# Weights of the experts split only at a change of expert, under branches on ScalarE and VectorE

## The chip, the cores and the metric

The kernel runs on one core of one Trainium2 chip. The metric is the time of one execution on the device, in microseconds (us). The engines are named as the profile names them: PE (TensorE, matmuls; PEld is its weight loads), DVE (VectorE), ACT (ScalarE), POOL (GpSimd) and SP (SyncE, which here mostly issues DMAs). A q behind an engine's name is its queue of instructions that do no arithmetic.

## The reference

Three layers in a row, all in float32. In the middle one each token goes to one of eight experts.

```python
# 1. causal attention with decay: 4 x 8 heads, 576 positions, 64 wide
scores = scale * q @ k.T + (cum[:, None] - cum[None, :])   # cum = cumsum(log(f))
x = softmax(where(causal, -1e9, scores)) @ v               # -> (2304, 512)
# 2. mixture of experts, top 1: w1 (8, 512, 1024), w2 (8, 1024, 512)
logits = x @ w_gate + modality_bias[modality_id]
e_idx = argmax(logits, axis=1)
for e in range(8):
    mask = e_idx == e
    h = maximum(x[mask] @ w1[e], 0.0)
    out[mask] = gate_w[mask, None] * (h @ w2[e])           # gate_w: softmax at e_idx
# 3. dense: w_in (512, 2048), w_out (2048, 512)
h = out @ w_in
y = maximum(0.01 * h, h) @ w_out
```

## The kernel before

Every float32 matmul of the last two layers is made of three: an operand is split into a high part (`..h`, rounded to the type that PE takes at full rate) and the rest (`..l`), and high by high, high by low and low by high are summed in PSUM. To split a tile takes a cast on ACT, `hi = raw`, and a subtraction on DVE, `lo = raw - hi`. Tiles are named so: `w1r`, `w1h`, `w1l` are the raw, high and low part of an expert's w1, four pieces of 128x1024 each; `w2r`, `w2h`, `w2l` the same of w2; `xh`, `xl` of the tokens of a slot, `hh`, `hl` of the hidden layer.

The attention runs first, 16 groups in 4 batches of tokens, and each batch is routed as it comes. The expert stage works on slots of 128 tokens of one expert. The first four slots (K1 = 4) are full slots out of the first three batches, so that the stage can begin before the last batch is routed; the other slots are laid out by `finish()` when all counts are known. There are at most 25 slots (NS); steps 0 to 17 are always run, the others under `tc.If(nr > t)`. With these inputs 20 slots run.

`step(t)` holds gemm1 of slot t (24 matmuls, four pieces k of w1), `trh(t-1)`, which transposes the hidden layer of the slot before, `trx`, which transposes the tokens of the next slot, and gemm2 of slot t-1 (24 matmuls). Inside a step the instructions of all five engines keep the order in which the code issues them (`ordered`), except that the work which `finish()` and the last routing issue, outside of it, is put between them by a scheduler with priorities. Each engine runs its own list in order and waits with semaphores.

In before, every step splits the eight weight pieces of the next slot, also where the expert stays the same (`split(t + 1, 0, k)` and `split(t, 1, k)`, L744 and L745). Each split is followed by the DMA of that piece for the slot after (L735), which is skipped when that slot has the same expert: `ei` holds the expert of each slot and `ni` whether it is new. `finish()` builds these tables, the slots (`slots`, `scan`), the stacked index tables (`per_token`, L511 and L513; `table`, L520 and L523) and the token indices of the other slots (L528 to L533: matmuls `tp`, then `tq`, `idt`, `gidx` on DVE), from which POOL gathers tokens (L740).

Of the kernel before, what the change touches and what calls it, by code (L numbers as in the profile page):

```python
# [9 lines left out]
F32 = mybir.dt.float32  # L10
F32R = mybir.dt.float32r
BF16 = mybir.dt.bfloat16
# [25 lines left out]
K1 = 4  # L38
# [9 lines left out]
SP = 2.0  # L48
TE = 3
TX = 3  # L50
RLAG = 8
# [29 lines left out]
def fused(ctx: ExitStack, tc, qk0, qk2, vp, f, mid, wg, mb, w1, w2, w_in, w_out, out):  # L81
# [29 lines left out]
    nc.gpsimd.iota(j128, [[P, NSTAT]], base=0, channel_multiplier=0, allow_small_or_imprecise_dtypes=True)  # L111
    col = cp.tile([P, P], F32, name="col")
    nc.gpsimd.iota(col, [[1, P]], base=0, channel_multiplier=0, allow_small_or_imprecise_dtypes=True)
# [15 lines left out]

    gidx, oidx, ei, ni = ([cp.tile([P, n] + d, I32, name=f"{c}{n}") for n in (K1, N2)] for c, d in (("gidx", []), ("oidx", [2]), ("ei", []), ("ni", [])))  # L130
    nt = cp.tile([P, 1], I32, name="nt")
# [11 lines left out]
    def at_slot(tiles, t):  # L143
        return tiles[t >= K1], t - K1 if t >= K1 else t
# [3 lines left out]
    with tc.tile_pool(name="pst", bufs=PST, space=PSUM) as pst:  # L148
# [351 lines left out]
        def slots(tp, n, inc):  # L500
# [38 lines left out]
        def route1(tp, m):  # L539
# [11 lines left out]
            gi, ef = slots(rt, K1, inc)  # L551
            nw = tp.tile([P, K1], F32, name="nw1")
            nc.vector.memset(nw, 1.0)
            nc.vector.tensor_tensor(nw[:, 1:], ef[:, 1:], ef[:, :K1 - 1], ALU.not_equal)
            nc.vector.tensor_scalar(ei[0], ef, float(E - 1), None, ALU.min)
            nc.vector.tensor_copy(ni[0], nw)
            yield
# [141 lines left out]
    with tc.tile_pool(name="rt2", reuse_waits="tile", bufs=1) as rt2, \  # L699
# [10 lines left out]
        ysc = []  # L710
        R = {}
        for t, c in ((xh, "h"), (xl, "l")):
            t.append(mw.tile([P, DM], F32R, name=f"x{c}1"))
# [4 lines left out]

        def regs(t):
            m, i = at_slot(ei, t)  # L720
            e = nc.sync.value_load(m[0:1, i:i + 1], min_val=0, max_val=E - 1)
# [5 lines left out]
            return e, cnd  # L727

        def load(t, which, k):
            if t not in R:  # L730
                R[t] = regs(t)
            e, cnd = R[t]
            raw, src = (w2r, w2) if which else (w1r, w1)
            o = raw[k].rearrange("p a b -> p (a b)") if which else raw[k]
            nc.sync.dma_start(o, src[bass.ds(e, 1), :, k * FF:(k + 1) * FF].rearrange("o p f -> (o p) f"), cond=cnd)  # L735
# [88 lines left out]
        def step(t):  # L824
            nx = t + 1 < NS
            if not t:
                split(t, 1, 0)
                split(t, 1, 1)
            keepg(t)
            if t == K1 - 1:  # L830
                next(fini)
            if t + 2 < NS and t + 2 != K1:
                gather(t + 2)
            gemm1(t, 0, 2)
            if not t:
                trx(1)
            aside(t, "load")
            if 0 < t < TE:
                trh(t - 1)
            if nx:  # L840
                split(t + 1, 0, 0)
            aside(t, "a1")
            aside(t, "a2")
            if t >= TE:
                trh(t - 1)
            if t > NSTAT:
                split(t - 1, 1, 2)
                split(t - 1, 1, 3)
            aside(t, "b")
            if nx:  # L850
                split(t + 1, 0, 1)
            aside(t, "pool")
            gemm1(t, 2, 3)
            if nx:
                split(t + 1, 0, 2)
            gemm1(t, 3, 4)
            keep(t)
            if nx:
                split(t + 1, 0, 3)
            if t:  # L860
                gemm2(t - 1, 0, 4)
            if nx and 0 < t < TX:
                trx(t + 1)
            if t:
                split(t, 1, 0)
                split(t, 1, 1)
            if nx and t >= TX:
                trx(t + 1)
            if t in (1, K1):
                next(fini, 0)  # L870
            aside(t, "d")
            if t:
                gemm2(t - 1, 4, 8)
            if t < NSTAT:
                split(t, 1, 2)
            if t:
                yout(t - 1)
            if t < NSTAT:
                split(t, 1, 3)

        def finish():
# [9 lines left out]
            gi, ef = slots(rt2, N2, inc)  # L891
            nw = rt2.tile([P, N2], F32, name="nw")
            nc.vector.tensor_tensor(nw[:, 1:], ef[:, 1:], ef[:, :N2 - 1], ALU.not_equal)
            nc.vector.tensor_tensor(nw[:, :1], ef[:, :1], early["ef"][:, K1 - 1:], ALU.not_equal)
            nc.vector.tensor_scalar(ei[1], ef, float(E - 1), None, ALU.min)
            nc.vector.scalar_tensor_tensor(ni[1], ef, float(E), nw, ALU.is_lt, ALU.mult)
# [45 lines left out]
        next(fini)  # L942
        with tc.issue_after(preps[-1].ins):
            for k in range(4):
                load(0, 0, k)
            gather(0)
            gather(1)
            for k in range(4):
                load(0, 1, k)
        with tc.high_priority():  # L950
            for k in range(4):
                split(0, 0, k)
        trx(0)
# [135 lines left out]
```

## Time and profile before

| | us |
|---|---|
| time, median of 3 runs (lowest, highest) | 940.06 (939.44, 940.16) |
| the profiled execution | 940.09 |
| its span | 938.4 |
| attention, about | 0 to 261 |
| steps of the expert stage, about | 261 to 524 |
| dense layer, about | 528 to 938 |
| PE, DVE, ACT, POOL busy | 871.3, 660.1, 504.3, 207.3 |

Times in the views are counted from the start of the span. A timeline row gives start, length, engine, line, operation, tiles and, in brackets, how long the engine idled before it and who released it. [...] Where an instruction overlaps the end of the one before, busy time counts the overlap once.

### The profile page before, as it was taken

What the parts mean: (1) busy time and instruction counts of PE and PEld (TensorE: products, weight loads), DVE (VectorE), ACT (ScalarE), POOL (GpSimd) and SP (SyncE); (2) the same over time, 40 slices, a digit from 0 to 9 for tenths busy, and PEclk for the clock granted to TensorE, in tenths of its full rate; (3) what the DMA queues carried; (4) which work ended last, traced back from release to release, by engine and by line L of the source; (5) the groups of instructions that cost most, each with busy time, mean ns of one, the idle gap of its engine ahead of it and who ended that gap; (6) DMA issues with size and microseconds to landing.
All of it is one profiled execution on the core that took longest, in us unless ns stands there. A gap on an engine that the chain in (4) does not pass through costs nothing. (4 is left out here: it accounts for less than half of the span.)

```text
span 938.4 us, 14476 instructions
## 1 busy us (share of the span) xinstructions
PE 871.3 (93%) x4733; PEld 715.2 (76%) x4733; DVE 660.1 (70%) x1203; ACT 504.3 (54%) x979; POOL 207.3 (22%) x161
## 2 busy tenths in 40 slices
PE   4888888889897999999999999999999999999996
PEld 2766666677676878888878778888888888888885
DVE  8877878679699999999998537348544953483333
ACT  5454555556685889999998445335222532242221
POOL 7433424242011234444443100000000000001112
PEclk9799999899898999999999999999999999999998
DMA  7666757765534842621132124004100420011111
GB/s 203 154 173 177 187 152 173 164 161 123 202 73 135 274 124 72 208 84 47 59 113 92 62 66 135 1 23 115 44 1 1 114 65 1 1 45 45 46 45 68
DMA packets 39754, 94.51 MB, mean 101 GB/s; under 512 B 14108, under 2 KB 14780, under 8 KB 39673
## 3 DMA queue, kind: packets, MB, share of 16 engines
q1 hardware_dynamic: 34872, 78.30, 30.3%
q0 software_dynamic: 4800, 15.23, 5.1%
q8 instruction: 39, 0.64, 0.3%
q14 instruction: 43, 0.34, 0.1%
HBM read 132.08 MB, written 14.99 MB: 157 GB/s over the span
## 5 line engine op out<-in xcount | busy, mean ns | idle before, releaser
L995 DVE SCALAR_TENSOR_TENSOR us<-u,us 128x512 f32<-128x512 f32 (+1 forms) x80 | 51.0, 638 | 125.5 <-ACT us L994 125.0
L994 ACT COPY us<-u 128x512 f32<-128x512 f32 (+1 forms) x80 | 43.5, 544 | 161.8 <-PE u L992 161.7
L992 PE MATMUL u<-fxl,whii 128*128 128x512 f32 (+1 forms) x320 | 118.1, 369 | 0.0
L992 PE MATMUL u<-fxh,wloi 128*128 128x512 f32 (+1 forms) x320 | 117.9, 368 | 0.0
L992 PE MATMUL u<-fxh,whii 128*128 128x512 f32 (+1 forms) x320 | 116.8, 369 | 0.7 <-ACT fxh L650 0.7
L1012 PE MATMUL a<-whio,gh 128*128 128x512 f32 x288 | 112.8, 392 | 0.0
L1012 PE MATMUL a<-wloo,gh 128*128 128x512 f32 x288 | 112.3, 390 | 0.0
L745 DVE TENSOR_TENSOR w1l<-w1r,w1h 128x1024 fp32r<-128x1024 f32 x84 | 101.0, 1223 | 8.5 <-ACT w1h L744 8.2
L1012 PE MATMUL a<-whio,gl 128*128 128x512 f32 x288 | 106.0, 390 | 0.0
L351 ACT ACTIVATE p<-sc,nm 128x128 f32<-128x128 f32 (+3 forms) x128 | 68.0, 535 | 61.1 <-DVE nm L348 48.3
L745 DVE TENSOR_TENSOR w2l<-w2r,w2h 128x1024 fp32r<-128x1024 f32 x80 | 94.4, 1218 | 0.9 <-ACT w2h L744 0.7
L1022 POOL DMA_INDIRECT out<-acc,tid x18 | 17.7, 984 | 327.4 <-DVE acc L1019 290.2
L744 ACT CAST w1h<-w1r 128x1024 fp32r<-128x1024 f32 x84 | 86.1, 1054 | 5.9 <-DMA w1r<-w 3.7
L744 ACT CAST w2h<-w2r 128x1024 fp32r<-128x1024 f32 x80 | 81.4, 1051 | 4.4 <-PE y L792 2.3
L999 DVE TENSOR_TENSOR gl<-us,gh 128x512 fp32r<-128x512 f32 (+1 forms) x80 | 50.9, 637 | 39.7 <-ACT gh L998 38.9
L998 ACT CAST gh<-us 128x512 fp32r<-128x512 f32 (+1 forms) x80 | 46.2, 578 | 58.4 <-DVE us L995 39.7
L792 PE MATMUL y<-w2h,hl 128*128 128x512 f32 x160 | 64.8, 405 | 5.3 <-DVE hl L785 5.3
L992 PEld LDWEIGHTS u<-fxh,whii 128*128 128x128 f32 x320 | 60.2, 188 | 11.1 <-ACT fxh L650 0.9
L992 PEld LDWEIGHTS u<-fxh,wloi 128*128 128x128 f32 x320 | 60.3, 188 | 10.4
L992 PEld LDWEIGHTS u<-fxl,whii 128*128 128x128 f32 x320 | 60.3, 188 | 10.3
L792 PE MATMUL y<-w2h,hh 128*128 128x512 f32 x160 | 66.0, 412 | 0.0
L792 PE MATMUL y<-w2l,hh 128*128 128x512 f32 x160 | 63.9, 399 | 0.0
(262 smaller groups left out, 1945.3 us busy)
## 6 DMA issues: line engine op xcount, KB each, us to landing
w1r<-w SPq DMA_DIRECT2D x88, 512.0 KB
w2r<-w SPq DMA_DIRECT2D x82, 512.0 KB
aq<-hi SPq DMA_DIRECT2D x30, 288.0 KB
rwi<-w_in SPq DMA_DIRECT2D x16, 512.0 KB
rwo<-w_out SPq DMA_DIRECT2D x16, 512.0 KB
raw<-qk SPq DMA_DIRECT2D x14, 576.0 KB
vt<-vp SPq DMA_DIRECT2D x16, 320.0 KB
xr<-yd SPq DMA_DIRECT2D x18, 256.5 KB
```

The costliest lines, as they stand in the source:

```text
L351: nc.scalar.activation(pt[:, :n], view[:, i, :], AF.Exp, bias=nm[:, i:i + 1], scale=1.0, accum_out=sms[g % 3][:, c, j:j + 1])
L744: nc.scalar.copy(hi[k], raw[k])
L745: nc.vector.tensor_tensor(lo[k], raw[k], hi[k].bitcast(F32), ALU.subtract)
L792: nc.tensor.matmul(Yp[t], lhsT=ap[:, k * P:(k + 1) * P], rhs=wp[k // 2][:, k % 2, :], start=(k == 0 and i == 0), stop=(k == NFB - 1 and i ...
L992: nc.tensor.matmul(ps, lhsT=w[:, c], rhs=x[:, k, :], start=(k == 0 and i == 0), stop=(k == NKB - 1 and i == 2))
L994: nc.scalar.copy(us, ps)
L995: nc.vector.scalar_tensor_tensor(us, ps, 0.01, us, ALU.mult, ALU.max)
L998: nc.scalar.copy(gh, us)
L999: nc.vector.tensor_sub(gl, us, gh.bitcast(F32))
L1012: nc.tensor.matmul(A[b][i], lhsT=x[:, c], rhs=w, start=(first and m == 0), stop=(last and m == 2))
L1022: d = nc.gpsimd.indirect_dma_start(out=out[:, :], out_offset=bass.IndirectOffsetOnAxis(ap=tid[:, c:c + 1], axis=0), in_=Y[b, i], in_offset ...
```

## The change

The weights of a slot are split only where its expert differs from that of the slot before. `finish()` and the early routing make flags on the chip: `nwa` (1 where the expert is new), packed into two integers by `bits()` with the powers of two `pw`. ACT and DVE load such an integer into a register and branch on one bit per slot and weight (`resplit`). Inside the branch stand the four splits; the cast of piece 0 is on DVE now, the other three on ACT. Where the branch is not taken, the engine adds to its semaphore what the splits would have added. The raw buffers hold the next other expert of the list (`en`), loaded where `ln` says so, right behind the split that frees them.

In `step`, the splits, which stood one by one between the matmuls, become one `resplit` for w1 of the next slot behind the last gemm1, and one for w2 at the end. `trh(t-1)` comes before the third piece of gemm1 in every step, `trx(t+1)` between the third and the fourth, and gemm2 is issued whole. The tail has no splits. `col`, an input of the routing's one-hot tables `lall`, becomes bf16. The core of the diff:

```diff
-    col = cp.tile([P, P], F32, name="col")
+    col = cp.tile([P, P], BF16, name="col")
...
+        def bits(tp, i, a, b):
+            u = tp.tile([P, b - a], F32, name=f"bu{i}")
+            nc.vector.tensor_tensor(u, nwa[:, a:b], pw[:, :b - a], ALU.mult)
+            r = tp.tile([P, 1], F32, name=f"br{i}")
+            nc.vector.tensor_reduce(r, u, axis=AX.X, op=ALU.add)
+            nc.vector.tensor_copy(nb[i], r)
...
+        def load(t, which, k):
+            raw, src = (w2r, w2) if which else (w1r, w1)
             cnd = None
-            if t:
-                m, i = at_slot(ni, t)
-                n = nc.sync.value_load(m[0:1, i:i + 1], min_val=0, max_val=1)
+            if t < 0:
+                e = first
+            else:
+                if t not in R:
+                    e = nc.sync.value_load(en[0:1, t:t + 1], min_val=0, max_val=E - 1)
+                    R[t] = e, nc.sync.value_load(ln[0:1, t:t + 1], min_val=0, max_val=1)
+                e, n = R[t]
                 cnd = (n != 0)
...
-        def split(t, which, k):
+        def split(which, k):
             raw, hi, lo = (w2r, w2h, w2l) if which else (w1r, w1h, w1l)
-            nc.scalar.copy(hi[k], raw[k])
+            if k == 0:
+                nc.vector.tensor_copy(hi[k], raw[k])
+            else:
+                nc.scalar.copy(hi[k], raw[k])
             nc.vector.tensor_tensor(lo[k], raw[k], hi[k].bitcast(F32), ALU.subtract)
-            if t + 1 < NS:
-                load(t + 1, which, k)
+        def resplit(t, which):
+            p = t >= K1
+            if p not in WD:
+                WD[p] = nc.values_load(nb[p][0:1, 0:1], engines=SPLITTERS, min_val=0, max_val=2 ** (N2 if p else K1) - 1)
+            with tc.If(((WD[p] >> (t - K1 * p)) & 1) != 0):
+                for k in range(4):
+                    split(which, k)
+            for k in range(4):
+                load(t, which, k)
...
             aside(t, "load")
-            if 0 < t < TE:
+            if t:
                 trh(t - 1)
-            if nx:
-                split(t + 1, 0, 0)
             aside(t, "a1")
             aside(t, "a2")
-            if t >= TE:
-                trh(t - 1)
-            if t > NSTAT:
-                split(t - 1, 1, 2)
-                split(t - 1, 1, 3)
+            gemm1(t, 2, 3)
+            if nx and t:
+                trx(t + 1)
             aside(t, "b")
-            if nx:
-                split(t + 1, 0, 1)
             aside(t, "pool")
-            gemm1(t, 2, 3)
-            if nx:
-                split(t + 1, 0, 2)
             gemm1(t, 3, 4)
             keep(t)
+            if not t:
+                for k in range(4):
+                    split(1, k)
+                    load(0, 1, k)
             if nx:
-                split(t + 1, 0, 3)
+                resplit(t + 1, 0)
             if t:
-                gemm2(t - 1, 0, 4)
-            if nx and 0 < t < TX:
-                trx(t + 1)
-            if t:
-                split(t, 1, 0)
-                split(t, 1, 1)
-            if nx and t >= TX:
-                trx(t + 1)
+                gemm2(t - 1, 0, 8)
             if t in (1, K1):
                 next(fini, 0)
             aside(t, "d")
             if t:
-                gemm2(t - 1, 4, 8)
-            if t < NSTAT:
-                split(t, 1, 2)
-            if t:
                 yout(t - 1)
-            if t < NSTAT:
-                split(t, 1, 3)
+                resplit(t, 1)
...
+            bits(rt2, 1, K1, NS)
             nc.vector.tensor_scalar(nt, inc[:, E - 1:E], float(K1), None, ALU.add)
+
+            wn, wx = (rt2.tile([P, NS], F32, name=n) for n in ("wn", "wx"))
+            nc.vector.tensor_scalar(wn, nwa, -BIG, BIG, ALU.mult, ALU.add)
+            nc.vector.tensor_add(wn, wn, efa)
+            nc.vector.scalar_tensor_tensor(wn, slott, float(E), wn, ALU.mult, ALU.add)
+            for a, b in ((0, NS // 2), (NS // 2, NS)):
+                sn = [P, b - a, NS]
+                m = m2.tile([P, XW], F32, tag="ys", name=f"bh{a}")[:, :(b - a) * NS].rearrange("p (t s) -> p t s", s=NS)
+                nc.gpsimd.memset(m, BIG)
+
+                nc.gpsimd.affine_select(m, m, [[1, b - a], [-1, NS]], ALU.is_ge, 0.0, a, 0)
+                nc.vector.tensor_tensor(m, m, wn.unsqueeze(1).to_broadcast(sn), ALU.add)
+                nc.vector.tensor_reduce(wx[:, a:b], m, axis=AX.X, op=ALU.min)
+            nc.vector.tensor_copy(en, wx)
+            nc.vector.tensor_scalar(en, en, E - 1, None, ALU.bitwise_and)
+            nc.vector.scalar_tensor_tensor(ln, wx, BIG, nwa, ALU.is_lt, ALU.mult)
...
         with tc.high_priority():
             for k in range(4):
-                split(0, 0, k)
+                split(0, k)
+        for k in range(4):
+            load(0, 0, k)
         trx(0)
```

What this moves, shown at three places. First DVE where the stage begins. `hl` of slot 0 is what gemm2(0) needs; `h2` is the last table of `finish()`. Before:

```order
L462 TENSOR_REDUCE pf3_3266<-ps_3_3263 128x5 [waits DVE_49]
L886 TENSOR_TENSOR gt_3365<-runb_96,j128_85 128x144 [waits DVE_49]
L785 TENSOR_TENSOR hl_3362<-th0_0_3565,hh_3361 128x512 [waits Activation_49]
L785 TENSOR_TENSOR hl_3362<-th0_1_3572,hh_3361 128x512 [waits Activation_49]
L465 CAST pi3_3269<-pf3_3266 128x5 [waits DVE_49]
L888 TENSOR_REDUCE nsl_3367<-gt_3365 128x8 [waits DVE_49]
L745 TENSOR_TENSOR w1l0_2902<-w1r0_119,w1h0_129 128x1024 [waits DMAHW0_49,Activation_49]
L745 TENSOR_TENSOR w1l1_2903<-w1r1_120,w1h1_130 128x1024 [waits DMAHW1_49,Activation_49]
L466 TENSOR_SCALAR pi3_3269<-pi3_3269 128x5 [waits DVE_49]
L889 TENSOR_TENSOR nsl_3367<-nsl_3367,used_2758 128x8 [waits DVE_49]
L745 TENSOR_TENSOR w1l2_2904<-w1r2_121,w1h2_131 128x1024 [waits DMAHW2_49,PE_49,Activation_49]
L467 TENSOR_SCALAR pi3_3269<-pi3_3269 128x5 [waits DVE_49]
```

After, from the end of `finish()` on (`h2`), with the first branch, that for w1 of slot 1:

```order
L544 TENSOR_TENSOR h2_3438<-h121_3436,idf_94 128x20x21
L774 TENSOR_LOAD en0_105 [waits DVE_49]
L775 REGISTER_ALU x2
L775 COMPARE_AND_BRANCH
L765 CAST w1h0_137<-w1r0_127 128x1024 [waits DMAHW4_49]
L768 TENSOR_TENSOR w1l0_2914<-w1r0_127,w1h0_137 128x1024 [waits DVE_49]
L768 TENSOR_TENSOR w1l1_2915<-w1r1_128,w1h1_138 128x1024 [waits DMAHW5_49,Activation_49]
L768 TENSOR_TENSOR w1l2_2916<-w1r2_129,w1h2_139 128x1024 [waits DMAHW6_49,Activation_49]
L768 TENSOR_TENSOR w1l3_2917<-w1r3_130,w1h3_140 128x1024 [waits DMAHW7_49,Activation_49]
L775 UNCONDITIONAL_BRANCH
L775 UNCONDITIONAL_BRANCH [waits DVE_49]
L817 TENSOR_TENSOR hl_3374<-th0_0_3619,hh_3373 128x512 [waits Activation_49]
```

Before, `hl` of slot 0 stood among the first instructions of `finish()` (`gt`, `nsl`), with the w1 splits of slot 1 after it. Now all of `finish()` up to the table `h2`, and the first branch, stand ahead of it.

Second, PE at the start of gemm1(1); `h1` is its result, `rk` the counts of the last batch. Before:

```order
L764 MATMUL h0_3479<-w1h3_132,xl0_134 128x512 x2
L764 MATMUL h0_3479<-w1l3_2905,xh0_133 128x512 x2
L764 MATMUL h1_3552<-w1h0_129,xh1_3359 128x512 [waits PE_49,Activation_49]
L764 MATMUL h1_3552<-w1h0_129,xh1_3359 128x512
L764 MATMUL h1_3552<-w1h0_129,xl1_3360 128x512 [waits DVE_49]
L764 MATMUL h1_3552<-w1h0_129,xl1_3360 128x512
L764 MATMUL h1_3552<-w1l0_2902,xh1_3359 128x512 [waits DVE_49]
```

After:

```order
L471 MATMUL rk3_3267<-oall_146,onesb_70 128x24
L471 LDWEIGHTS onesb_70
L471 MATMUL rk3_3267<-oall_146,onesb_70 128x16
L775 UNCONDITIONAL_BRANCH
L796 MATMUL h1_3606<-w1h0_137,xh1_3371 128x512 [waits DVE_49,Activation_49]
L796 MATMUL h1_3606<-w1h0_137,xh1_3371 128x512
L796 MATMUL h1_3606<-w1h0_137,xl1_3372 128x512 x2
L796 MATMUL h1_3606<-w1l0_2914,xh1_3371 128x512 [waits DVE_49]
```

Before, the first matmul of `h1` waited for PE and ACT. Now the counts of the last batch come ahead of it, and it waits for DVE too: for the count of pieces that DVE reaches in the first branch, or with the sum that it adds when it passes it.

Third, DVE near the end of the attention, where the first expert's w1 arrives; `xub` is what PE multiplies next. Before:

```order
L523 TENSOR_TENSOR h2_2867<-h14_2865,idf_94 128x15x4
L397 COPY xub_185<-pv13_1_2978 128x192 [waits PE_49]
L408 TENSOR_SCALAR rr14_3169<-sm2_175 128x10 [waits Activation_49]
L409 RECIPROCAL rr14_3169<-rr14_3169 128x10 [waits DVE_49]
L348 TENSOR_REDUCE nm15_0_0_2990<-sc15_0_0_2991 128x2 [waits PE_49]
L745 TENSOR_TENSOR w1l0_2902<-w1r0_119,w1h0_129 128x1024 [waits DMAHW4_49,DMAHW5_49,DMAHW2_49,Activation_49]
```

After:

```order
L544 TENSOR_TENSOR h2_2879<-h14_2877,idf_94 128x15x4
L765 CAST w1h0_137<-w1r0_127 128x1024 [waits DMAHW2_49]
L411 COPY xub_193<-pv13_1_2990 128x192 [waits PE_49]
L422 TENSOR_SCALAR rr14_3181<-sm2_183 128x10 [waits Activation_49]
L768 TENSOR_TENSOR w1l0_2914<-w1r0_127,w1h0_137 128x1024 [waits DMAHW5_49,DMAHW4_49,DVE_49]
L362 TENSOR_REDUCE nm15_0_0_3002<-sc15_0_0_3003 128x2 [waits PE_49]
```

The cast of the first piece, which waits for its DMA, now stands on DVE, ahead of the copy `xub`.

## Rows read from the trace of the kernel before

**Rows 1.** The page: its first two lines.

```profile
span 938.4 us, 14476 instructions
PE 871.3 (93%) x4733; PEld 715.2 (76%) x4733; DVE 660.1 (70%) x1203; ACT 504.3 (54%) x979; POOL 207.3 (22%) x161
```

**Rows 2.** Windows of some stretches: busy microseconds (instructions) of each engine, then granted clock.

```profile
core 0: us, PE busy (x) PEld busy (x) DVE busy (x) ACT busy (x) POOL busy (x), PEclk, DMA share, GB/s
292.64:297.07 4.43, 4.43 (x10) 3.36 (x11) 4.43 (x5) 0.00 (x0) 0.00 (x0) 0.50 0.72 193
350.00:475.00 125.00, 125.00 (x608) 103.09 (x607) 123.12 (x137) 115.57 (x152) 56.46 (x30) 1.00 0.31 95
519.20:522.60 3.40, 3.40 (x11) 2.62 (x10) 2.88 (x4) 3.09 (x5) 0.00 (x0) 0.50 0.21 80
239.25:246.00 6.75, 6.75 (x41) 6.10 (x41) 5.67 (x12) 4.74 (x9) 0.00 (x0) 0.50 1.00 396
```

**Rows 3.** The waits of PE, in 262:330, 330:470 and 470:535: total, times, longest.

```profile
PE y L792 <- DVE hl L785: 5.1, 2, 4.8
...
PE h L764 <- DVE xl L754: 1.1, 1, 1.1
...
PE th L782 <- DVEq L962: 1.9, 1, 1.9
PE h L764 <- DVE xl L754: 1.0, 1, 1.0
```

**Rows 4.** Timeline of PE about gemm1(1): start, length, instruction.

```profile
266.97 0.63 PE L764 MATMUL h<-w1h,xh 128*128 128x512 f32 x2
...
269.31 0.19 PE L452 MATMUL rk<-oall,before 128*128 128x32 bf16 x1
...
269.68 0.71 PE L764 MATMUL h<-w1l,xh 128*128 128x512 f32 x2
...
300.41 1.37 PE L528 MATMUL tp<-h,lall 128*128 128x42 bf16 x20
```

**Rows 5.** Timeline of DVE in the same stretch.

```profile
265.60 0.68 DVE L754 TENSOR_TENSOR xl<-tx,xh 128x512 fp32r<-128x512 f32 x1
...
274.07 1.28 DVE L785 TENSOR_TENSOR hl<-th,hh 128x512 fp32r<-128x512 f32 x2
...
285.00 0.33 DVE L503 TENSOR_TENSOR gi<-slott,scan 128x168 f32<-128x168 f32 x1
...
289.12 0.60 DVE L520 TENSOR_TENSOR h<-slott,stk 128x420 bf16<-128x420 f32 x1
```

**Rows 6.** Windows of DVE alone, in two pieces without a split.

```profile
283.40:286.53 3.13, 3.13 (x25) 1.00 0.00 0
287.67:290.77 3.10, 2.90 (x11) 0.95 0.22 85
```

**Rows 7.** Groups by line and form: count, busy and mean ns, idle before.

```profile
L745 DVE TENSOR_TENSOR w1l<-w1r,w1h 128x1024 fp32r<-128x1024 f32 x84 | 101.0, 1223 | 8.5 <-ACT w1h L744 8.2
L298 DVE CAST hi<-raw 128x1152 fp32r<-128x1152 f32 x14 | 10.6, 758 | 13.9 <-DMA bk<-hi 6.1 <-DMA bk<-agd 2.9 <-DMA bq<-bq 1.8
```

**Rows 8.** Timelines of ACT, PE and DVE in the attention tail.

```profile
237.77 1.04 ACT L744 CAST w1h<-w1r 128x1024 fp32r<-128x1024 f32 x1 [3.35 <-DMA w1r<-w]
...
239.25 1.00 PE L528 MATMUL tp<-h,lall 128*128 128x8 bf16 x15 [3.20 <-ACT tt L381]
...
234.04 0.35 DVE L397 COPY xub<-pv 128x192 f32<-128x192 f32 x1
```

**Rows 9.** Register loads and compares by line: count, then ns min/median/max.

```profile
L958 DVEq TENSOR_LOAD <-nt x1: 542/542/542, 491.8 to 491.8; - x1
...
L962 PEldq COMPARE_BRANCH  x4: 65/142/3803, 486.8 to 516.3; - x4
L962 DVEq COMPARE_BRANCH  x4: 43/51/67, 492.4 to 517.9; - x4
```

**Rows 10.** The gathers by line: from issue to landing.

```profile
DMA to landing us min/median/max: 3.4/5.1/10.1
```

More of the change, by code (lines that the diff above doesn't have):

```diff
@@ L48 @@
 SP = 2.0
-TE = 3
-TX = 3
 RLAG = 8
@@ L127, in fused @@
     wgs = cp.tile([P, NKB, E], F32, name="wgs")
-    gidx, oidx, ei, ni = ([cp.tile([P, n] + d, I32, name=f"{c}{n}") for n in (K1, N2)] for c, d in (("gidx", []), ("oidx", [2]), ("ei", []), ("ni", [])))
+    gidx, oidx = ([cp.tile([P, n] + d, I32, name=f"{c}{n}") for n in (K1, N2)] for c, d in (("gidx", []), ("oidx", [2])))
+    en0 = cp.tile([P, 3], I32, name="en0")
+    e0 = en0[:, 0:1]
+    en = cp.tile([P, NS], I32, name="en")
+    ln = cp.tile([P, NS], I32, name="ln")
+    nb = [en0[:, 1:2], en0[:, 2:3]]
+    pw = cp.tile([P, NS], F32, name="pw")
+    nc.gpsimd.memset(pw[:, 0:1], 1.0)
+    w = 1
+    while w < NS:
+        m = min(w, NS - w)
+        nc.gpsimd.tensor_scalar(pw[:, w:w + m], pw[:, :m], float(2 ** w), None, ALU.mult)
+        w += m
+    efa = cp.tile([P, NS], F32, name="efa")
+    nwa = cp.tile([P, NS], F32, name="nwa")
     nt = cp.tile([P, 1], I32, name="nt")
@@ L551, in route1 @@
             gi, ef = slots(rt, K1, inc)
[L552 to L556, printed above, removed]
+            nc.vector.memset(nwa[:, 0:1], 1.0)
+            nc.vector.tensor_tensor(nwa[:, 1:K1], ef[:, 1:], ef[:, :K1 - 1], ALU.not_equal)
+            nc.vector.tensor_scalar(efa[:, :K1], ef, float(E - 1), None, ALU.min)
+            nc.vector.tensor_copy(e0, efa[:, 0:1])
+            bits(tp, 0, 0, K1)
             yield
@@ L711, in fused @@
         R = {}
+        WD = {}
+        SPLITTERS = (mybir.EngineType.Activation, mybir.EngineType.DVE)
         for t, c in ((xh, "h"), (xl, "l")):
@@ L717, in fused @@
         oc = mw.tile([P, 2], I32, name="oc")
-        def regs(t):
-            m, i = at_slot(ei, t)
-            e = nc.sync.value_load(m[0:1, i:i + 1], min_val=0, max_val=E - 1)
+        def load(t, which, k):
+            raw, src = (w2r, w2) if which else (w1r, w1)
             cnd = None
-            if t:
-                m, i = at_slot(ni, t)
-                n = nc.sync.value_load(m[0:1, i:i + 1], min_val=0, max_val=1)
-                cnd = (n != 0)
[L727 to L733, printed above, removed]
+            if t < 0:
[5 more added lines that the diff above has]
+                e, n = R[t]
+                cnd = (n != 0)
             o = raw[k].rearrange("p a b -> p (a b)") if which else raw[k]
@@ L825, in step @@
             nx = t + 1 < NS
-            if not t:
-                split(t, 1, 0)
-                split(t, 1, 1)
             keepg(t)
@@ L872, in step @@
             if t:
-                gemm2(t - 1, 4, 8)
-            if t < NSTAT:
-                split(t, 1, 2)
-            if t:
                 yout(t - 1)
-            if t < NSTAT:
-                split(t, 1, 3)
+                resplit(t, 1)
         def finish():
@@ L891, in finish @@
             gi, ef = slots(rt2, N2, inc)
-            nw = rt2.tile([P, N2], F32, name="nw")
+            nw = nwa[:, K1:]
             nc.vector.tensor_tensor(nw[:, 1:], ef[:, 1:], ef[:, :N2 - 1], ALU.not_equal)
             nc.vector.tensor_tensor(nw[:, :1], ef[:, :1], early["ef"][:, K1 - 1:], ALU.not_equal)
-            nc.vector.tensor_scalar(ei[1], ef, float(E - 1), None, ALU.min)
-            nc.vector.scalar_tensor_tensor(ni[1], ef, float(E), nw, ALU.is_lt, ALU.mult)
+            nc.vector.tensor_scalar(efa[:, K1:], ef, float(E - 1), None, ALU.min)
+            nc.vector.scalar_tensor_tensor(nw, ef, float(E), nw, ALU.is_lt, ALU.mult)
+            bits(rt2, 1, K1, NS)
             nc.vector.tensor_scalar(nt, inc[:, E - 1:E], float(K1), None, ALU.add)
+            wn, wx = (rt2.tile([P, NS], F32, name=n) for n in ("wn", "wx"))
[12 more added lines that the diff above has]
+            nc.vector.scalar_tensor_tensor(ln, wx, BIG, nwa, ALU.is_lt, ALU.mult)
             nc.vector.tensor_sub(exc, exc, used)
@@ L943, in fused @@
         with tc.issue_after(preps[-1].ins):
+            first = nc.sync.value_load(e0[0:1, 0:1], min_val=0, max_val=E - 1)
             for k in range(4):
-                load(0, 0, k)
+                load(-1, 0, k)
             gather(0)
@@ L948, in fused @@
             for k in range(4):
-                load(0, 1, k)
+                load(-1, 1, k)
         with tc.high_priority():
             for k in range(4):
-                split(0, 0, k)
+                split(0, k)
+        for k in range(4):
+            load(0, 0, k)
         trx(0)
```

2 lines of the change are left out of this document (removed).

## Prediction

> **What bounds the kernel now.** I read the page first, then the table by stage, the waits of TensorE in order of time, and the timelines around each. The page gives a span of 938.4 us with PE busy 871.3, so 67 us is all that PE idles, and DVE 660.1 [rows 1]. In the steady part of the expert stage, 350 to 475 us, PE is busy 125.00 of 125.00, DVE 123.12 and ACT 115.57 [rows 2]: PE sets the pace, and the splits that the change removes lie under it. Freeing DVE and ACT there gives nothing. What can be won is where PE waits. In the whole expert stage that is one long wait at its start, 4.8 us for `hl` (5.1 with the short one before it), and 1.1, 1.0 and 1.9 us later [rows 3], plus what the clock takes after the long ones: behind the 4.8 us wait PE runs 4.43 us at half the granted clock (1.2 GHz), behind the 1.9 us wait 3.40 us, and in the attention tail 6.75 us [rows 2]. Half of such a stretch is lost. So before loses 5.1 + 2.2 = 7.3 us at the start of the stage and 1.1 + 1.0 + 1.9 + 1.7 = 5.7 us behind it.
>
> **The steady part.** Expert counts worked out from the reference's inputs are 49, 1083 and 1172 tokens for experts 1, 2 and 5 and none for the others. The 20 slots that run hold experts 2 (four times), 1, 2 (five times), 5 (ten times), so the new flags are set at slots 0, 4, 5 and 10. Of 84 and 80 split pairs 16 and 16 stay. By rows that is 68 + 64 subtractions of 1.22 us [rows 7] less on DVE, and about as many casts less on ACT, all beside a full PE: 0 us. At a switch the four splits come in one burst on DVE, one cast and four subtractions, 0.67 + 4 x 1.22 = 5.6 us (the cast scaled from 0.758 us for 1152 columns to 1024 [rows 7]); the burst for w1 lies beside gemm2, the one for w2 beside gemm1, each about 5.6 us or more of PE. I take 0 for the three switches, with 0 to 1 us each as bounds.
>
> **The start of the stage, where I expect the loss.** The flag branches are written into the program in order. The first one, for the w1 of slot 1, is issued in step 0, and every DVE instruction that was written before it stands ahead of it: the four w2 splits of slot 0, the rest of the routing, and the whole first part of `finish()`. Before, gemm1(1) needed only the refreshed `w1h` and `w1l` pieces, and `hl` of slot 0 stood in the middle of that list, at 274.07 [rows 5]. Now PE's first matmul of gemm1(1) waits for DVE, and what it waits for is the piece count that DVE adds only when it has passed this branch, split or no split. So an unchanged expert no longer frees PE early: gemm1(1) stands behind `finish()`.
>
> When does DVE get there? It starts the list behind `xl` of slot 1, which ends at 266.3 [rows 5]; a w2 subtraction that stood ahead of it is gone, so 265.8. The list:
> - w2 of slot 0: 5.6 us as above.
> - The routing and `finish()` work that was there already. Its two unbroken pieces are 25 instructions in 3.13 us and 11 in 3.10 us [rows 6]. Six of the 25 move behind the branch, which leaves 2.4; some 13 more stood one by one between splits, at 3.13 / 25 = 0.125 us each 1.6. Together 7.1.
> - New: nine narrow instructions, 0.125 us each if they follow closely and 0.2 if each waits for the one before, 1.1 to 1.8; and two additions and two reductions of 300 or 325 columns, between 0.33 us for 168 columns and 0.60 for 420 [rows 5], about 0.47 each, 1.9. Together 3.0 to 3.7, I take 3.2. The bf16 `col` may give back up to 0.5 on `lall`.
>
> That is 15.9 - 0.3 = 15.6 us, so 281.4. The register load is 0.54 us and the compare 0.05 [rows 9]; the jump past the split, the drain and the jump back are in no row; I take 0.5 (0.1 to 2). PE gets its first matmul of gemm1(1) at about 282.5. It was due at 266.97, now 0.37 later since the `rk` matmuls stand ahead of it (269.31 to 269.68 before) [rows 4]: 267.3. The wait is 15.2 us. The clock falls after it too; the loss is bounded by the two stretches seen, 4.43 / 2 = 2.2 and 6.75 / 2 = 3.4, I take 2.8. The start then loses 18.0 us where it lost 7.3: **+10.7 us**. `hl` itself is no wait any more, since by then DVE has nothing else. Queued behind the branch on DVE are `hl` of slot 0, `xl` of slot 2 and the indices of the early slots; all are wanted by PE only after gemm1(1).
>
> [...]
>
> **The attention tail.** The first w1 cast goes from ACT to DVE and stands there ahead of the `xub` copy. Before, ACT's cast waited 3.35 us for its load, until 237.77, while the copy on DVE was done at 234.4; PE waited 3.20 us for ACT's next copy, until 239.25 [rows 8]. Now both engines stand behind that load, ACT with the second piece. DVE frees `xub` at 237.77 + 0.67 + 0.35 = 238.8, no later than PE's present wait, but ACT's piece lands later, and the row maximum that ACT needs comes behind a subtraction. Bounds 0 and 1.5; I take **+0.8 us**.
>
> **The gather of slot 4.** trx(4) moves from the middle of gemm2(2) to before the last quarter of gemm1(3), 5 us or so earlier behind the index matmuls that end at 301.8 [rows 4]. A gather takes 3.4 to 10.1 us to land, 5.1 in the middle [rows 10], and is issued a microsecond behind the indices. 0 to 3; **+0.7 us**.
>
> **The gains behind.** With no splits queued, `xl` in the early and last steps is not late: -1.1 and -1.0; the 1.9 us at the end of the slots is DVE finishing splits of a slot that isn't there, and its half-clock stretch goes with it: -1.9 - 1.7 [rows 2, 3]. The nested branches keep some of it: I take **-5.2 us** of 5.7.
>
> The sum is 10.7 + 0.8 + 0.7 - 5.2 = +7.0 us. The profiled execution took 940.09 us, 1.7 more than its span, and the median of the runs is 940.06, so nothing is to be added for that: 947.1, rounded to **947.0 us**.
>
> **The rivals.**
> - Faster: DVE passes the first branch early enough that the wait at gemm1(1) costs less than the one at `hl` did. Each microsecond earlier is one off the time: the kernel is even with before at 282.5 - 7.0 = 275.5 and faster beyond doubt from 273.6 on. At 272.5 it would take 937.0. For it: before, the narrow instructions stood between splits, so their length back to back is partly inferred, and with no long instruction among them they may overlap more. Against: the four subtractions, 4.9 us, and the two unbroken pieces, 5.5 us, are measured, and these alone bring the end to 276.2. I keep 0.12 for it, mostly for a misreading of what gemm1(1) waits for, and 0.10 for a time within 0.2% of before.
> - Slower still: control flow costs on every step. PE has two jumps in each step, some 39 that run, ACT and DVE two compares and jumps. If each PE jump showed with 0.2 us (twice a compare of this trace, an estimate), 39 x 0.2 = 8 us: 955. Against: PE's compare rows are 65 to 142 ns [rows 9], and three steps with such branches ran before with no other PE wait than the listed ones [rows 3]; the targets lie a few rows away. [...] A list longer by 3 us or a longer half-clock stretch gives 948 to 950 alone and 952 together. Chance 0.12.
> - The change does not do what it says (flags wrong, splits kept everywhere): then the start is as forecast and the gains behind are gone, 947.0 + 5.2 = 952. Counted with the slower case; nothing in the code speaks for it.
>
> **How the numbers follow.** The forecast has 0.66, its own range is 942 to 951. About 0.2% (1.9 us) is what a measurement of this kernel can tell from no change. Slower by more: 0.66 + 0.12 = 0.78; within: 0.10; faster: 0.12. The range leaves out the faster case and the far end of the slower one: 938.5 to 952.
>
> **What would show it.** Right: in the waits of PE one entry of 13 to 17 us at the first matmul of gemm1(1), released by DVE's branch line, with PE at half clock behind it; no wait for `hl` at gemm2(1); DVE under half busy between 350 and 475 us with PE still full; the th wait at the tail gone. The DVE timeline should show the flag's register load near 281 us. Wrong: gemm1(1) starting before 275, a wait at each step, or a switch step longer than its neighbours by more than 1 us.

## The result, and the profile after

The changed kernel takes 944.61 us (median of 16 runs, 941.07 to 951.05), the kernel before on the same chip 938.94 (16 runs, 931.51 to 946.16). The ratio is 1.0072, with a 95% interval of 1.0048 to 1.0095: slower by 0.7%, or 6.8 us (4.5 to 8.9) of 938.94, where +7.0 us was forecast. The two medians alone differ by 5.7 us.

The first two lines of the page answer to [rows 1]:

```profile
span 942.1 us, 14355 instructions
...
PE 866.0 (92%) x4733; PEld 713.0 (76%) x4733; DVE 521.2 (55%) x1095; ACT 375.2 (40%) x839; POOL 168.8 (18%) x171
```

DVE lost 139 us of work and ACT 129, and the span grew by 3.7. The windows of the changed kernel, in the columns of [rows 2], show why the work was worth nothing: PE is as full without it. (Third from the end stands the clock granted to PE as a share of the full one, behind it the busy share of the DMA engines and what they moved.)

```profile
279.62:284.40 4.78, 4.78 (x11) 3.77 (x12) 0.00 (x0) 0.00 (x0) 0.00 (x0) 0.50 0.77 253
350.00:475.00 125.00, 125.00 (x608) 103.51 (x608) 46.74 (x68) 48.95 (x80) 23.72 (x31) 1.00 0.27 77
```

The waits of PE, in 250:330, 330:470 and 470:535 (total, times, longest), answer to [rows 3]:

```profile
PE h L796 <- DVEq L775: 13.4, 1, 13.4
PE tx L784 <- DMA xg<-xs,gidx: 1.2, 1, 1.2
...
PE y L824 <- DVE hl L817: 1.8, 1, 1.8
...
PE th L814 <- ACTq L992: 1.4, 1, 1.4
```

The long one is no longer for `hl` at gemm2(1). It is for DVE's sequencer (DVEq) at the line of the new branch, at the first matmul of gemm1(1). The timeline of DVE, ahead of that branch, answers to [rows 5]; between the first and the last row shown it hardly stands still:

```profile
264.44 0.68 DVE L765 CAST w2h<-w2r 128x1024 fp32r<-128x1024 f32 x1
265.16 1.22 DVE L768 TENSOR_TENSOR w2l<-w2r,w2h 128x1024 fp32r<-128x1024 f32 x1
...
267.93 1.23 DVE L768 TENSOR_TENSOR w2l<-w2r,w2h 128x1024 fp32r<-128x1024 f32 x1 [0.22 <-ACT w2h L767]
...
271.73 0.93 DVE L487 TENSOR_SCALAR lall<-col,pq 128x128 bf16<-128x128 bf16 x5
...
275.73 0.88 DVE L920 TENSOR_TENSOR bh<-bh,wn 128x300 f32<-128x300 f32 x2
...
276.61 0.86 DVE L921 TENSOR_REDUCE wx<-bh 128x12 f32<-128x300 f32 x2
...
278.31 1.10 DVE L544 TENSOR_TENSOR h<-h,idf 128x420 bf16<-128x420 bf16 x2
```

And PE's timeline behind it, to be held against [rows 4]:

```profile
279.62 1.19 PE L796 MATMUL h<-w1h,xh 128*128 128x512 f32 x2 [13.36 <-DVEq L775]
280.61 1.05 PE L796 MATMUL h<-w1h,xl 128*128 128x512 f32 x2
```

DVE's list runs from 264.44 to 279.41; PE goes on at 279.62, after 13.36 us of idling, and at a granted clock of 0.50 for 4.78 us (the first window above). Its matmuls of 512 columns start 0.427 us apart there, 1.2 columns a nanosecond, which the prediction writes as 1.2 GHz; at 1.00 they start 0.23 us apart.

The chain from slot to slot can be followed in one number per slot, the start of the first weight load (PEld) of its gemm1. Slot 1 is left out, since before its matmuls follow those of slot 0 without a break. "Dense" is the first weight load of the dense layer.

| us | slot 0 | 0 to 2 | 2 to 3 | 3 to 4 | 4 to 7 | 7 to 18 | 18 to 19 | 19 to dense |
|---|---|---|---|---|---|---|---|---|
| before | 260.87 | 19.33 | 21.51 | 12.28 | 39.10 | 136.52 | 13.67 | 24.27 |
| after | 259.62 | 34.50 | 13.87 | 13.66 | 39.10 | 135.85 | 12.32 | 22.49 |
| difference | -1.25 | +15.17 | -7.64 | +1.38 | 0.00 | -0.67 | -1.35 | -1.78 |

The start of the stage (slots 0 to 3) costs +7.53, the gather of slot 4 +1.38, and the rest gives 3.80 back, net. The 0.00 of slots 4 to 7 hides two things: after has the new `hl` wait of 1.8 us there, and has lost the `xl` wait of 1.1 us and smaller ones. The first column is noise: the profiles of six kernels with the same attention code start slot 0 anywhere between 255.6 and 263.6.

### The profile page after: what moved, and what is told of

Same layout as the page of the kernel before. It is cut to its first block, busy times and chain, and to the rows that moved or that the text cites. A ratio compares the mean times of both kernels' runs of the same rounds, so it can differ in the third digit from the quotient of the medians.

```text
span 942.1 us, 14355 instructions
## 1 busy us (share of the span) xinstructions
PE 866.0 (92%) x4733; PEld 713.0 (76%) x4733; DVE 521.2 (55%) x1095; ACT 375.2 (40%) x839; POOL 168.8 (18%) x171
## 5 line engine op out<-in xcount | busy, mean ns | idle before, releaser
L817 DVE TENSOR_TENSOR hl<-th,hh 128x512 fp32r<-128x512 f32 x40 | 25.7, 685 | 118.4 <-ACT hh L816 118.4
L796 PE MATMUL h<-w1h,xh 128*128 128x512 f32 x160 | 54.5, 423 | 13.4 <-DVEq L775 13.4
L824 PE MATMUL y<-w2h,hl 128*128 128x512 f32 x160 | 62.6, 391 | 1.8 <-DVE hl L817 1.8
L1042 PEld LDWEIGHTS a<-whio,gl 128*128 128x128 f32 x288 | 54.1, 188 | 11.5
L824 PE MATMUL y<-w2h,hh 128*128 128x512 f32 x160 | 62.7, 392 | 0.0
L359 PE MATMUL sc<-ak,aq 128*128 128x128 f32 (+3 forms) x128 | 52.4, 417 | 10.7 <-ACT p L351 4.7
```

Source lines behind the costliest of these rows:

```text
L359: nc.tensor.matmul(view[:, i, :], lhsT=aq[:, j, qs], rhs=ak[:, j, :n], start=(i == 0), stop=False)
L796: nc.tensor.matmul(Hp[t][:, n, :], lhsT=xp[t % 2][:, k * P:(k + 1) * P], rhs=wp[k][:, n * 512:(n + 1) * 512], start=(k == 0 and i == 0), s ...
L817: nc.vector.tensor_sub(hl[:, c], ps, hh[:, c].bitcast(F32))
L824: nc.tensor.matmul(Yp[t], lhsT=ap[:, k * P:(k + 1) * P], rhs=wp[k // 2][:, k % 2, :], start=(k == 0 and i == 0), stop=(k == NFB - 1 and i ...
L1042: nc.tensor.matmul(A[b][i], lhsT=x[:, c], rhs=w, start=(first and m == 0), stop=(last and m == 2))
```

## The experiments

Their times are medians, and their ratios are to the kernel before, run beside them on the same chip. Stretches, waits and clocks come from one profiled execution of each. The theory is that of the prediction: what costs is DVE's list ahead of the first branch. The main rival is that branches cost where they stand.

**1. No branches.** The three switches of these inputs are fixed in the program; the flags are still made, but nothing branches on them.

```diff
-            with tc.If(((WD[p] >> (t - K1 * p)) & 1) != 0):
+            if t in (4, 5, 10):
```

> The branches and the register loads are taken out of the changed kernel and replaced by the outcome that they have for these inputs: splits at slots 0, 4, 5 and 10, none elsewhere. My theory (the first branch is a wall behind which gemm1(1) waits for all of finish()): the 13.4 us wait and the 2.4 us of half clock behind it go, hl of slot 0 comes at about 272, so some 15.5 us less than the changed kernel, about 929. The rival that the jumps themselves cost time in each of the 19 steps behind: the steps shorten too, by 0.2 us and more each, 4 to 8 us on top, and it beats e2 by as much. By my theory e1 and e2 are within 1 us of each other, but for up to 1.4 us at the end of the slots.

930.21 us, ratio 0.992 (0.9896 to 0.9945), where about 929 was forecast. Slot 0 to 2 takes 18.67 us, and the wait at gemm1(1) is gone. The same splits without branches are faster than before: the idea of the change is sound, its price lies in the branches' places.

**2. Only the first branches away.** Branches stay from slot 4 on; those of slots 1 to 3, whose expert doesn't change here, are left out with their splits.

```diff
-            with tc.If(((WD[p] >> (t - K1 * p)) & 1) != 0):
...
+            if p:
...
+                with tc.If(((WD[p] >> (t - K1 * p)) & 1) != 0):
```

> Branches and splits of slots 1 to 3 alone are left out of the changed kernel (with these inputs the four early slots share an expert); those of slots 4 to 24 stay. My theory: the whole loss at the start goes, 13.4 + 2.4 = 15.8 us, since the first branch now stands in step 3, long after finish(); about 929. Rival A (the jumps cost on every step): only 6 of some 39 branches are gone, so it gains little beyond the wait and stays 4 to 8 us above e1. Rival B (finish() has to run before something else early, such as the loads or gather of slot 4): the wait comes back further on, at hl of slot 1 or at the transposes of slot 4, and less than 8 us are won.

931.4 us, 0.9947 (0.9921 to 0.9972). Slot 0 to 2 takes 18.71, and slot 0 to slot 19 236.54 us against 236.72 with no branch at all. Slots 7 to 18, in which each step has its branches here and none in experiment 1, take 135.85 in both. So some thirty PE jumps and as many on ACT and DVE cost nothing that can be seen; the rival falls. The whole rest of its difference to experiment 1 lies from slot 19 on: 26.74 against 22.27 us. That led to experiment 7.

**3. The first cast back on ACT.** Piece 0 of a split is cast by ScalarE again.

```diff
-            if k == 0:
-                nc.vector.tensor_copy(hi[k], raw[k])
-            else:
-                nc.scalar.copy(hi[k], raw[k])
+            nc.scalar.copy(hi[k], raw[k])
```

> The cast of piece 0 goes back to ACT; all else as in the changed kernel. My theory: the list in front of the first branch gets shorter by one cast, 0.68 us, and so does the wait at gemm1(1), 13.4 to 12.7; the 1.8 us wait for hl at a change of expert falls to about 1.1. In the attention tail ACT now stands behind the load earlier, ahead of an exponential; there it may lose up to 2 us. Together -1.4 to +1 us. The rival that the cast on DVE is what costs most in the change (through the attention tail and through DVE's bursts): 3 us or more faster than the changed kernel.

944.39 us, 1.0077 (1.0045 to 1.0109). Slot 0 to 2 took 33.71, 0.8 less than after: about the length of the one cast (0.68) taken off the list. PE now waits in two pieces:

```profile
PE h L793 <- DVEq L772: 7.4, 1, 7.4
PE h L793 <- ACTq L772: 4.6, 1, 4.6
```

First it waits for ACT's own jump, then for DVE's; the sum, 12.0, is little below 13.4. So the cast's place is not the cause of the wait. The time itself tells less than it seems to: slot 19 to dense takes 26.83 here, 4.3 more than after, by a long jump on ACT (see 7), and that can hide a gain elsewhere. A gain in the attention tail is not excluded: the last 350 matmuls ahead of slot 0 took 48.2 us here, 50.2 after, and 47.9 to 53.4 in the six profiles whose attention code differs from this one in that cast alone.

**4. A longer list.** The two wide reductions of `finish()` are done five times each.

```diff
-                nc.vector.tensor_reduce(wx[:, a:b], m, axis=AX.X, op=ALU.min)
+                for _ in range(5):
+                    nc.vector.tensor_reduce(wx[:, a:b], m, axis=AX.X, op=ALU.min)
```

> Each of the two wide reductions in finish() is done five times instead of once: 8 more on DVE at 0.43 us, 3.4 us in front of the first branch; the result is the same. My theory: one for one, the wait at gemm1(1) goes from 13.4 to 16.8 us and the time up by 3.4 us. The rival that gemm1(1) waits for something else that ends near there (ACT's branch, a load, the registers): DVE has slack and the time rises by less than 1 us.

945.31 us, 1.0096 (1.0065 to 1.0127). Slot 0 to 2 went from 34.50 to 37.89, +3.39, the figure forecast, but by a sum of three parts. DVE's list (261.54 to 279.57) is 3.06 us longer than after's. PE goes on 1.40 us behind its end where after has 0.21, so the wait rose by 4.25, to 17.61, and not by 3.4:

```profile
280.97 1.19 PE L796 MATMUL h<-w1h,xh 128*128 128x512 f32 x2 [17.61 <-DVEq L775]
```

And the half clock behind it lasts 3.2 us, not 4.78, which gives 0.8 back. The wait follows the list, so the rival that something else ends there falls. The times don't decide it: the median is 0.7 us above the changed kernel's, where 3.4 was forecast and under 1 by the rival, and the two intervals overlap.

The 1.40 us come from what stood last on the list. The register load of the flag, then the compare (first of two loads and of 45 compares in each row), after:

```profile
L774 DVEq TENSOR_LOAD <-en x2: 306/428/551, 278.3 to 315.9; - x2
L775 DVEq COMPARE_BRANCH  x45: 43/56/72, 279.1 to 516.4; - x45
```

and here:

```profile
L774 DVEq TENSOR_LOAD <-en x2: 306/429/552, 279.4 to 316.3; - x2
L775 DVEq COMPARE_BRANCH  x45: 43/56/72, 280.2 to 516.9; - x45
```

After ends its list with the two long rows of `h2`, 1.10 us, and both load and compare began before these were done, at 279.41. Here three operations of 0.18 us stood last: the load began 0.2 us before the list's end, at 279.57, and the compare behind it.

**5. A later list.** Every branch and flag stays, but `finish()` is cut in three and its parts are emitted behind the first branches.

```diff
+            if nx:
+                resplit(t + 1, 0)
             if not t:
                 for k in range(4):
                     split(1, k)
                     load(0, 1, k)
-            if nx:
-                resplit(t + 1, 0)
...
+            if t == 1:
+                for _ in held[-1]:
+                    pass
+                next(fini)
```

(The first branch so moves ahead of the four w2 splits of slot 0 too, which were 5.6 us of the list in the forecast. `held[-1]` is the rest of the last routing; the table of next experts follows in step 2 ahead of `resplit(3, 0)`, the token table behind it. The early loads take a small table of the early slots, since the full one comes later.)

> All jumps and flags stay; finish() is cut in three and its parts are emitted behind the jump on w1 of slot 1 (the counts and the second flag word at the end of step 1, the next-expert table in step 2, the token table in step 2), and the loads of slots 0 to 2 take the next slot of the early table. Theory (the list, not the jumps, is what costs): slot 0 to slot 2 as in the version with the first jumps left out, 18.7 us and not 34.5, the wait at gemm1(1) gone, no half clock there; in steps 1 and 2 VectorE has 8 to 9 us of index work beside 2 to 6 us of other work in 12.3 us, so 0 to 2 us new wait for hl; the gather of slot 4 is waited for 2.4 to 2.6 us, as whenever the slots start early. Time about 931 (928 to 934), below both kernels. Rival (the jumps themselves, or the list wherever it stands, cost): time moved to steps 1 to 3, slot 0 to slot 4 still over 55 us (after 62.0, first jumps left out 47.6), time 938 to 944.

933.75 us, 0.9961 (0.9935 to 0.9987): faster than before, by less than forecast. The 13.4 us wait is gone, but slot 0 to 2 took 22.23, not 18.7, and slot 2 to 3 17.41 where experiment 2 has 13.87. PE's timeline names the two waits, neither of them foreseen:

```profile
264.43 0.71 PE L809 MATMUL h<-w1h,xh 128*128 128x512 f32 x2 [1.83 <-ACTq L788]
...
294.32 1.37 PE L558 MATMUL tp<-h,lall 128*128 128x42 bf16 x20 [3.37 <-DVEq L788]
```

The first is ACT's jump, which stands behind the relu of slot 0. The second is the token table: its matmuls on PE stand ahead of gemm1(3), and DVE makes their operand too late. The foreseen gather wait didn't come: behind the second wait the clock dips (0.71 from 294.32 to 298 us), and PE takes 8.0 us from these matmuls to the transposes of slot 4's rows, at 302.34, where it had 6.65 after (from 306.70 to 314.57, less the wait of 1.22) and the gather landed in time.

**6. The two later waits.** On top of 5, the second index list moves from step 4 to the end of step 3, and `trx(4)` behind half of gemm2(2).

```diff
+            if t == K1 - 1:
+                gemm2(t - 1, 0, 4)
+                trx(t + 1)
+                gemm2(t - 1, 4, 8)
...
                 resplit(t, 1)
+            if t == K1 - 1:
+                next(fini, 0)
```

> The version with the late finish(), and with it two moves: the second index list (oid(1)) is emitted at the end of step 3 and not in step 4, and the transposes of slot 4's rows stand behind the first half of gemm2(2) and not between the parts of gemm1(3). Theory: the wait for hl in the step of the switch goes from about 1.8 to under 0.4 us (2.3 us of index work no longer stand ahead of it on VectorE), the wait for the gather from 2.4 to 2.6 to under 0.3 us (3.8 us more PE work ahead of it): 3.5 to 4 us below the version with the late finish() alone, about 927. Rival: the two waits only move on (the w2 splits of slot 4 end no earlier because the raw w2 comes late, xh and xl of slot 4 become late): 0 to 1 us.

930.16 us, 0.9908 (0.9874 to 0.9943). The `hl` wait of 1.8 us is gone and slot 5 to 6 takes 12.38 us, not 14.52. The median is 3.6 us below experiment 5's, as forecast, but only this 2.1 us is the edit's: in the traces the other gain is slot 0 to 2, 20.66 for 22.23, where the same wait was not followed by a lower clock (last section). The edit doesn't touch that stretch. The other half of the edit shows nothing, since experiment 5 had no gather wait to take away. The wait of 3.37 us stands as before.

**7 and 8. ACT's last jump.** At the end of the slots ACT jumps over the five that don't run. In the trace, from its compare to the next instruction, that takes 0.46 us after, 0.70 before and in experiment 1, but 2.43 in experiment 2 and 2.54 in 3. Both kernels add only small copies on ACT in steps 5 to 17: 7 has seven a step on top of experiment 2, and 8 has eight a step on top of the changed kernel. They ask whether the place of the jump in the program decides how long it takes; that it does was a guess of mine, from which a short jump was forecast for 7 and a long one for 8.

```diff
             keep(t)
+            if 5 <= t < 18:
+                for _ in range(7):
+                    nc.scalar.copy(pad, pw[:, 0:1])
```

> The version with the first jumps left out, with 91 copies of one column added on ScalarE in steps 5 to 17 (7 a step), nothing else. [...] The copies cost nothing in the steps, where ScalarE is busy 40%. Rival (the length of the jump in instructions or the state of the run decides, not the position): jump 2.4 again, time unchanged or some tenths longer.

929.26 us, 0.9915 (0.988 to 0.9951). The jump takes 0.42 us. PE at the end of the slots, in experiment 2:

```profile
508.52 1.97 PE L815 MATMUL th<-ident,hs 128*128 128x128 f32 x8 [3.37 <-ACTq L993]
```

and here:

```profile
508.38 1.09 PE L816 MATMUL th<-ident,hs 128*128 128x128 f32 x8 [1.36 <-ACTq L997]
```

At the end of the slots two microseconds less of waiting saved 4.25 us (slot 19 to dense 22.49, not 26.74): behind 3.37 us of idling the clock fell, behind 1.36 it didn't. The windows behind the two waits, of experiment 2 and of this one (granted clock third from the end):

```profile
508.52:514.00 5.48, 5.48 (x19) 4.91 (x20) 2.08 (x3) 1.76 (x3) 0.37 (x2) 0.50 0.10 37
```

```profile
508.38:513.00 4.62, 4.62 (x25) 3.62 (x26) 1.89 (x3) 1.56 (x3) 1.02 (x1) 1.00 0.17 64
```

Of these 4.25 us the whole run shows about half: slot 3 to 4 took 1.9 us more than in experiment 2 (the gather's wait was 3.0 us, not 2.6), and the medians differ by 2.1, with intervals that overlap.

> [...] Theory: the jump takes 2.4 to 2.5 us where it took 0.46, the wait of th at the end goes from 1.4 to about 3.4, slot 19 to the dense layer from 22.5 to 24.5 or more: about 2 us slower than the changed kernel by the trace. Rival (position decides nothing): jump 0.5, no difference in any stretch.

943.15 us, 1.0036 (1.0009 to 1.0063). The jump took 0.46 us as without the copies, and slot 19 to dense 22.54: a miss. So the place of the code may decide, as 7 suggests, but not in the way that I had guessed. Two kinds of jump exist in these runs, 0.4 to 0.7 and 2.4 to 2.5 us; what makes one long is not shown. Each program was profiled once, so whether one and the same program takes both kinds isn't shown either.

**9. The version that the experiments point to.** On top of 6, the relu of slot 0 goes behind the jump, and each part of the index work a step or a branch earlier, into gaps that DVE has.

```diff
-            keep(t)
-            if t == 2:
+            if t:
+                keep(t)
+            if t in (1, 2):
                 next(fini)
             if nx:
                 resplit(t + 1, 0)
             if not t:
+                keep(t)
...
+                for _ in held[-1]:
+                    pass
```

> The version with both moves, and three more: the relu of slot 0 (keep(0)) is emitted behind ScalarE's jump on w1 of slot 1 and not ahead of it, the rest of the last routing already at the end of step 0, the counts in step 1 ahead of the jump on w1 of slot 2, the next-expert table in step 1 behind it, the token table's one-hots in step 2 ahead of the jump on w1 of slot 3. Theory: TensorE's wait of 3.4 us for VectorE's jump at the token table goes to under 0.5 us (about 8 us of index work are done a step earlier), its wait of 1.8 us for ScalarE's jump at gemm1(1) to 0.6 us (the relu of 1.2 us is no longer ahead of the jump); slot 0 to slot 4 from 51.8 to about 47.2 us, the time about 925.5 (ratio 0.986 to before). Rival (the index work only moves the wait: to hl of slot 0 or 1, or to gemm1(2) behind the jump on w1 of slot 2): slot 0 to slot 4 still 50 to 52, time 929 to 930.

927.67 us, 0.9883 (0.9852 to 0.9913), below both kernels; 925.5 was forecast. Slot 0 to 4 takes 47.01 us (62.03 after, 53.12 before), where 47.2 was forecast. What PE still waits for in 250:330:

```profile
PE y L837 <- DVE hl L830: 0.9, 1, 0.9
PE h L809 <- DVEq L788: 0.8, 1, 0.8
PE pv L406 <- DVE xu L412: 0.2, 1, 0.2
```

The waits of 3.4 and 1.8 us are gone; 1.7 us of new ones stand in their place. All flags and branches that handle other inputs are still in it.

## Why the prediction was right, step by step

**The steady part, 0 us: right.** 350 to 475 us is full on PE before and after, and experiments 1 and 2 show no price of the branches there (slot 7 to 18: 135.85 in both and after, 136.52 before).

**The start, +10.7 us: right in kind, too large in size.** The mechanism is shown from both sides: a list 3.06 us longer made the wait 4.25 us longer (experiment 4), taking the branch away frees gemm1(1) (1, 2), and so does taking the list from in front of it (5). The sizes: the list was 15.0 us (forecast 15.6), the two wide additions and two reductions 1.74 of it (1.9). With the shorter type of `col` the five `lall` operations took 0.93 us, 1.06 before (median of one 0.242 and 0.286 us; one of after's took 0.410), so 0.13 of the possible 0.5 came back. The branch was mis-sized: 1.1 us of register load and jump were forecast, 0.5 of it for jumps that no row showed, and PE went on 0.21 us behind the list. The load began at 278.3 and the compare at 279.1, and the list ended at 279.41, so the 551 ns of the load were spent under the list. Experiment 4 shows the term's other face, 1.40 us, where the load isn't covered. The wait was 13.36 us (15.2) and the clock loss 4.78 / 2 = 2.4 (2.8): 15.8 lost. Before lost more here than forecast: slots 0 to 3 took 40.84 us where experiment 2 took 32.58, so 8.3, not 7.3; one microsecond of that is in no listed wait, and its cause is open. That leaves 7.5 where 10.7 stood. No single term carries the miss: before's loss has 1.0 of it, the branch 0.9, the list 0.6, the clock 0.4, and the list's earlier start, measured against when PE was due, 0.3.

**The attention tail, +0.8: not settled.** PE's waits there are 1.5 and 1.4 us where one of 3.20 stood [rows 8], with 0.75 for `xu` behind them where 0.16 stood, and slot 0 starts 1.25 us earlier. The start moves by several microseconds between profiles of the same code, so neither sign is shown (experiment 3 has the spread).

**The gather, +0.7: right in kind.** 1.22 us of wait; 2.4 and 2.6 in experiments 1 and 2, where the slots start earlier and the gather has less time.

**The switches, 0: one of three was wrong.** At slot 5's step `hl` was 1.8 us late, and slot 5 to 6 took 14.47 us where an undisturbed step takes 12.31: one of the signs that the prediction had named for being wrong. The bounds of 0 to 1 had the burst of w2 beside gemm1 alone; DVE's timeline has the index work and a weight of the dense layer in front of it:

```profile
334.64 0.16 DVE L947 TENSOR_TENSOR d<-used 128x7 f32<-128x7 f32 x1
...
336.93 0.68 DVE L703 SCALAR_TENSOR_TENSOR wvi<-rwi,wvi 128x512 int32<-128x512 int32 x1
337.54 0.69 DVE L765 CAST w2h<-w2r 128x1024 fp32r<-128x1024 f32 x1
338.26 4.63 DVE L768 TENSOR_TENSOR w2l<-w2r,w2h 128x1024 fp32r<-128x1024 f32 x4
342.80 1.28 DVE L817 TENSOR_TENSOR hl<-th,hh 128x512 fp32r<-128x512 f32 x2
```

From 334.64 to 336.93 only the index work runs; experiment 6 moved it and the wait went, and with it 2.1 us of slot 4 to 7 (37.01 for 39.10).

**The gains behind, -5.2: about 5.9 came.** The table's 3.80 are net of the 2.1 us lost at slot 5's step; with these added back, 5.9. The `xl` waits are gone. At the end of the slots the half-clock stretch went, as forecast, but the wait itself only fell from 1.9 to 1.40 and changed its releaser: DVE's late splits before, ACT's jump now. A branch that ends the slots was there in both; that it would be next in line was missed, and with it the sign "the th wait at the tail gone".

**The sum** was +7.0 and the comparison of many runs gave +6.8. The mechanism was right; that the numbers agree so closely is luck. The profiled pair differs by 3.7 us, and its ledger is the start +7.5 (10.7 forecast), the gather +1.4 (0.7), the switches +2.1 (0), the gains -5.9 (-5.2) and the start of slot 0 -1.25, which is noise (+0.8). The rival "faster" needed the first branch passed by 273.6; DVE passed it at 279.5. Of the rival with a price at every branch nothing is left. The prediction read PE's compares against it as 65 to 142 ns; the row goes on to 3803 [rows 9], so that reading left out the longest. That near targets make cheap jumps, as its argument there takes for granted, no run shows. What settles it is the 135.85 us above.

## What to carry to other kernels

Work taken off engines that stand beside a full one was worth nothing here (350 to 475 us: DVE busy 46.74 us, not 123.12, and PE 125.00 in both); what the change adds to the order of the program is worth what it makes the full engine wait. A branch on an in-order engine was a wall, for 13.36 us here: everything written ahead of it on that engine was waited for by PE, which waited for its passing, though the split inside was skipped. So set the branch before the long list or move the list behind it. After the repair look at what is next in line, and mend those waits one by one; here they were the relu, the token table and the index list.

## What the runs showed of the hardware that I had not expected

- The same jump on ACT takes 0.42 to 0.70 us in nine of these programs and 2.43 and 2.54 in two (experiments 2 and 3), where PE waited 3.4 and 3.5 us for it. With 91 idle copies added it was a short one, and the end of the slots 4.25 us shorter in the trace; whether the place of the code decides is not settled.
- Half the clock behind a wait isn't certain. [rows 2] and the stretches above show it behind 1.9, 3.4, 4.8 and 13.4 us. Behind 1.4 us of idling at the end of the slots PE kept a granted clock of 1.00 (508.38 to 513 us in experiment 7), behind 3.4 it ran 5.48 us at 0.50 (experiment 2). But the same wait of 1.83 us at gemm1(1) was followed by full clock in experiment 6 and by a mean of 0.61 over 3.07 us in 5, of which these are the windows (5 first):

```profile
264.43:267.50 3.07, 3.07 (x9) 2.39 (x10) 3.04 (x4) 2.98 (x4) 0.00 (x0) 0.61 0.01 2
```

```profile
263.10:266.20 3.10, 3.10 (x15) 2.52 (x16) 3.07 (x4) 2.98 (x4) 0.00 (x0) 1.00 0.01 3
```

- A register load of a flag cost nothing where DVE still worked on what stood ahead of it: PE went on 0.21 us behind the list in the changed kernel, and 1.40 us behind it in experiment 4, where the load was not covered.
